# Two rounds of attention and FFN for four tokens on one core: shorter norm and row sums, q and every gate and up as shifted row strips, last down projection over four column groups, all orders new

## The chip, the cores and the metric

The kernel runs on one core of a Trainium2 chip. The metric is the device time of one execution in microseconds, taken as the median of several runs. Five engines work beside each other, each with an instruction queue of its own: TensorE (PE, with its weight loads shown as PEld), VectorE (DVE), ScalarE (ACT), GpSimd (POOL) and SyncE (SP). SP and ACT issue the transfers between memory and the core's buffers. An engine executes its queue in order, so an instruction that waits holds up everything behind it on that engine.

## The reference

Four tokens (B = 4, one position each, width D = 448) go twice through the same attention and the same FFN, with the same weights and the same caches in both rounds.

```python
def _A_ref(x, k_cache, v_cache, wq, wo):
    B, Sq, D = x.shape
    Hq, Dh = 16, 256
    Hkv, Sk = k_cache.shape[1], k_cache.shape[2]
    W = min(4096, max(256, Sk // 4))
...
    k = jnp.repeat(k_cache[:, :, Sk - W:, :], rep, axis=1)
    v = jnp.repeat(v_cache[:, :, Sk - W:, :], rep, axis=1)
    scores = jnp.einsum("bhqd,bhkd->bhqk", q, k) * (Dh ** -0.5)
    p = _softmax(scores, axis=-1)
    o = jnp.einsum("bhqk,bhkd->bhqd", p, v)
...
x = A_x
x = x + _A_ref(_layernorm(x, axis=-1), A_k_cache, A_v_cache, A_wq, A_wo)
x = x + _B_ref(_layernorm(x, axis=-1), B_w_gate, B_w_up, B_w_down)
x = x + _A_ref(_layernorm(x, axis=-1), A_k_cache, A_v_cache, A_wq, A_wo)
x = x + _B_ref(_layernorm(x, axis=-1), B_w_gate, B_w_up, B_w_down)
```

`_B_ref` is `(silu(x @ w_gate) * (x @ w_up)) @ w_down` with an inner width of 1792. There are 8 key/value heads, two query heads to each, a window W of 2048 keys and a head width of 256. One token and head therefore needs 1 MiB of K and 1 MiB of V.

## The kernel before

**Work items.** A head of one token in one layer is one item, written as three digits (token, layer, head). `PLAN` lists 44 stages of one to three items. For an item the kernel loads K in two halves of 512 KB (or one transfer of 1 MB, for items in `WHOLE`) and V in two halves. DVE transposes each K half in 32x32 blocks (L841), POOL spreads the query (L880), PE makes the scores (L874), a softmax runs over DVE, PE and ACT (L890 to L930), PE multiplies by V (L952), ACT and DVE fold the parts (L968, L970), and PE applies the output projection (rows, L1026, or columns, L1018, for the item that completes a token's layer).

**Buffers.** K and V halves live in 27 slots of 512 KB. `KEEP_K` and `KEEP_V` say how many heads of each token stay in their slots from the first layer to the second, so that they are not read twice: 21 heads of K and 18 of V in all, of which token 0 has 5 and 6. A load into a used slot waits for the last instruction that reads what the slot held. `SLOTS` gives the slot of each load, in the order of SP's queue. The weights have buffers of their own, `wq_sb` among them.

**Order.** All instructions are first collected in a graph with numbers; `SEQ_PE`, `SEQ_DVE`, `SEQ_ACT`, `SEQ_POOL` and `SEQ_SP` then give each engine's order by those numbers, and `schedule` and `_place_waits` add the waits. Entries `w1` to `w28` of `SEQ_PE` are fillers: a product with a zero vector over 512 columns (L1274), which changes nothing and keeps PE working. There are 339 of them.

**A token between two layers.** When all 8 heads of a token are done in layer 0, a chain follows that ends with the token's new queries. In this text it is called a *turn*; the four turns are T0 to T3, by token. Each goes through these steps:

- `rows`: the row sums of the output projection leave PSUM on ACT (L761, rounded to bf16), DVE makes the remainder (L763), PE turns both into columns (L771), DVE adds them to x (L775); the last item's column part is added by `residual` (L779).
- `norm`: two DVE sums with accumulation (L534, L537), a float32 product over the partitions on PE (L540), the centred x (L544), a copy of the moments (L546), the last 64 rows doubled (L548, L551), and three POOL instructions for the rate (L556, L558, L560).
- The FFN, in one of two forms. T0 and T3 use `ffn`, in columns: 56 products of a 128x128 weight block for gate and 56 for up (L720), tanh on ACT for each token (L731), L734 and L738 on DVE, 56 products for down (L748), and the sum into x (L756). T1 and T2 (`ROWF`) use `ffn_row`: gate and up as four groups of 4 rows by 512 columns (L656), tanh (L662), L664 and L666 over 512 columns, a turn to columns (L672), and the down projection added into the row sums in bank A (L684), so that `rows` has to run again for each token concerned. T2 takes token 0's second FFN along, T3 token 1's.
- `norm` again, and `qproj`: 32 products of 512 columns on four column groups (L594), two copies scaled by the rate (L600), two turns (L610), a copy (L617), a spread over the partitions (L625), and the copy to `qc` (L630).

**The end.** `finale` does the last FFN, for tokens 2 and 3, from a mean that is worked out ahead (L1051): centred x (L1073), its variance on PE (L1092) and the rate on POOL (L1098), gate and up in columns (L1117, L1128), tanh (L1149), L1152 and L1157, then x of all four tokens laid into rows (L1172) and the down projection of all 14 blocks in two column groups of 224 columns (L1182), one copy (L1188) and two stores with all four tokens (L1190).

## Time and profile before

| what | value |
|---|---|
| median of 3 runs | 287.29 us (287.08 to 287.34) |
| profiled execution, from first to last instruction | 290.4 us |
| instructions | 11178 |
| PE busy, of which fillers (L1274) | 251.9 us, 102.1 us |
| DVE busy, of which K transposes (L841) | 192.0 us, 105.4 us |
| ACT, POOL busy | 62.9 us, 82.8 us |
| read from memory | 105.48 MB |

The profile is of one execution with the profiler on; its span is 3.1 us above the timed median. A row of the timeline has the start and the length in us, the engine, the line of the kernel, the operation with what it writes and reads, the count of instructions merged in it and, in brackets, how long the engine sat idle before and what ended that. A row of the stretches has from:to, the length, the busy time of PE, PEld, DVE, ACT and POOL with their counts, the granted PE clock (1.00 is full speed), the mean busy share of the 16 transfer engines and the rate in GB/s.

### The profile page before, as it was taken

Reading aid. Unit: us, or ns where it says so; the run is one execution under the profiler, and the core shown is the slowest. Engines: PE = TensorE matmul, PEld = TensorE weight load, DVE = VectorE, ACT = ScalarE, POOL = GpSimd, SP = SyncE. Lnnn points to the kernel's source line nnn. Section 1 sums busy time; section 2 is a strip of 40 time slices with the busy share of each in tenths; the row PEclk is TensorE's granted clock in tenths of the full one; section 3 lists DMA queues with packets and bytes.
Section 4 is the critical chain, followed back from the end, with each engine's and each line's share of the span. In section 5 each row is a group of like instructions: output and inputs, shape, how many; then the busy total and the mean of one; then the engine's idle time right before and its main releaser. Section 6 shows DMA issues by size and latency. Waiting matters only on the chain.

```text
span 290.4 us, 11178 instructions
## 1 busy us (share of the span) xinstructions
PE 251.9 (87%) x4933; PEld 141.6 (49%) x4933; DVE 192.0 (66%) x594; ACT 62.9 (22%) x178; POOL 82.8 (29%) x233
## 2 busy tenths in 40 slices
PE   3989799899898999798989898988869988879976
PEld 1434344544474454354544544454536546745675
DVE  5527756547353895887867479959697679556532
ACT  0012011121202132213223122313323231223400
POOL 0071003031024224122423231605233162245231
PEclk9999889999999999999899999999999999999957
DMA  7999999999997999999999999999999999999800
GB/s 278 420 423 417 406 415 396 402 408 403 391 402 235 368 408 416 413 414 401 349 320 407 383 418 407 408 410 374 381 387 373 415 405 353 332 342 395 350 5 0
DMA packets 29192, 106.20 MB, mean 366 GB/s; under 512 B 2900, under 2 KB 7000, under 8 KB 26840
## 3 DMA queue, kind: packets, MB, share of 16 engines
q1 hardware_dynamic: 27424, 96.12, 85.3%
q10 hardware_dynamic: 1720, 9.37, 7.9%
q8 instruction: 38, 0.62, 0.9%
q14 instruction: 10, 0.08, 0.1%
HBM read 105.48 MB, written 0.00 MB: 363 GB/s over the span
## 4 chain that ended last, share of the span: by engine, by line
PE 42%; DMA 34%; DVE 16%; issue 2%; ACT 2%; SPq 2%; POOL 1%; DVEq 0%; ACTq 0%
DMA half<-in_A_k_cache_dram 29%; PE A L1274 13%; DVE half L841 10%; PE S L874 7%; PE Y L952 6%; DMA half<-in_A_v_cache_dram 5%; PE A L1026 2%; PE Z L720 2%; DVE oh L970 2%; PE Y L921 2%; PE Z L748 1%; ACT oh L968 1%; PE A L1018 1%; DVE tiny L890 1%; SPq L851 1%
## 5 line engine op out<-in xcount | busy, mean ns | idle before, releaser
L841 DVE STREAM_TRANSPOSE half<-half 128x1024 uint32<-128x1024 uint32 x86 | 105.4, 1233 | 12.2 <-DMA half<-in_A_k_cache_dram 12.1
L1274 PE MATMUL A<-identb,small 128*128 128x512 bf16 x339 | 102.1, 401 | 5.3 <-DVE A L434 4.8
L965 POOL TENSOR_TENSOR small<-small 128x2 f32<-128x2 f32 (+1 forms) x50 | 39.2, 789 | 57.3 <-DVE small L943 55.4
L952 PE MATMUL Y<-half,pT 128*4 128x256 bf16 (+1 forms) x992 | 43.3, 272 | 6.3 <-DMA half<-in_A_v_cache_dram 3.7
L874 PE MATMUL S<-half,qe 128*8 128x128 bf16 (+1 forms) x1600 | 41.6, 236 | 6.7 <-DVE half L841 2.3
L1274 PEld LDWEIGHTS A<-identb,small 128*128 128x128 bf16 x339 | 29.4, 104 | 33.1 <-issue 12.0
L874 PEld LDWEIGHTS S<-half,qe 128*8 128x8 bf16 x1600 | 28.9, 85 | 18.8 <-DVE half L841 4.5
L908 ACT ACTIVATE praw<-S,small 104x128 bf16<-104x128 f32 (+1 forms) x50 | 19.8, 397 | 82.2 <-DVE small L904 73.7
L880 POOL TENSOR_TENSOR qe<-qc,tiny 128x64 bf16<-128x64 bf16 x64 | 17.9, 293 | 51.1 <-PE S L874 37.5
L970 DVE SCALAR_TENSOR_TENSOR oh<-oh,small,Y 128x256 bf16<-128x256 bf16 x49 | 23.1, 472 | 13.4 <-ACT oh L968 12.9
L968 ACT ACTIVATE oh<-Y 128x256 bf16<-128x256 f32 x49 | 18.7, 382 | 49.0 <-PE Y L952 43.6
L952 PEld LDWEIGHTS Y<-half,pT 128*4 128x4 bf16 (+1 forms) x992 | 18.4, 83 | 17.8 <-DMA half<-in_A_v_cache_dram 5.4
L890 DVE TENSOR_REDUCE tiny<-S 104x1 bf16<-104x128 f32 (+1 forms) x50 | 15.9, 318 | 6.0 <-PE S L874 5.9
L930 ACT ACTIVATE pT<-Y 128x64 bf16<-128x64 f32 (+1 forms) x50 | 12.6, 252 | 33.0 <-PE Y L921 28.5
L1026 PE MATMUL A<-wo_sb,oT 128*4 128x448 bf16 x200 | 16.7, 352 | 1.8 <-DVE oT L1006 1.7
L556 POOL TENSOR_SCALAR st<-st 128x1 f32<-128x1 f32 x15 | 4.0, 265 | 48.0 <-DVE st L546 47.9
L904 DVE TENSOR_REDUCE small<-S 104x1 f32<-104x32 f32 x50 | 8.8, 179 | 11.8 <-PE S L898 11.4
L1212 POOL MEMSET oT<- 128x16 bf16 x40 | 4.1, 112 | 40.1 <-PE A L1026 30.5
L943 DVE TENSOR_REDUCE small<-Y 128x2 f32<-128x32 f32 (+1 forms) x50 | 9.3, 188 | 8.8 <-PE Y L938 8.5
L1006 DVE TENSOR_TENSOR oT<-Y,small 128x4 bf16<-128x4 f32 (+1 forms) x63 | 8.9, 154 | 6.8 <-PE Y L976 5.3
L976 PEld LDWEIGHTS Y<-tiny,oh 128*128 128x128 bf16 x98 | 6.7, 100 | 10.9 <-DVE oh L970 6.0
L976 PE MATMUL Y<-tiny,oh 128*128 128x2 bf16 (+1 forms) x98 | 9.7, 168 | 2.5 <-DVE oh L970 2.1
(181 smaller groups left out, 272.5 us busy)
## 6 DMA issues: line engine op xcount, KB each, us to landing
half<-in_A_v_cache_dram SPq DMA_DIRECT2D x90, 512.0 KB, 7.8
half<-in_A_k_cache_dram SPq DMA_DIRECT2D x55, 512.0 KB, 7.3
half<-in_A_k_cache_dram SPq DMA_DIRECT2D x10, 1024.0 KB, 13.5
half<-in_A_k_cache_dram ACTq DMA_DIRECT2D x5, 1024.0 KB, 23.4
wo_sb<-in_A_wo_dram SPq DMA_DIRECT2D x7, 448.0 KB, 16.0
wq_sb<-in_A_wq_dram ACTq DMA_DIRECT2D x2, 1024.0 KB, 8.8
wd_sb<-in_B_w_down_dram SPq DMA_DIRECT2D x1, 1568.0 KB, 15.6
wg_sb<-in_B_w_gate_dram SPq DMA_DIRECT2D x1, 1344.0 KB, 9.1
```

Source lines behind the costliest of these rows:

```text
L841: return e.transpose(a, a)
L874: last = e.matmul(Sb[s_][qd:qd + 8, 0:32 * 2 * J], lhsT=qe[q_][:, P, ce, :, :].rearrange("p a n -> p (a n)"), rhs=keys(kcs[P], J * x, J, c ...
L880: g.op(POOL, "qe", lambda e, P=P, t=t, kvh=kvh: e.tensor_tensor(qe[q_][:, P, :, :, :], qc[t][:, kvh, :, :].unsqueeze(2).broadcast_to([128, ...
L890: g.op(DVE, f"max{n}", lambda e: e.tensor_reduce(pmax[s_][0:R, :], Sb[s_][0:R, 0:N], AX.X, ALU.max), r=(f"s{s_}",), w=(f"pmax{s_}",), bank ...
L908: return e.activation(praw[0:R, 0:128 * n].rearrange("p (g r l) -> p g r l", g=2 * n, l=2), Sb[s_][0:R, 0:128 * n].rearrange("p (l g r) -> ...
L952: last = e.matmul(Yb[p_][32 * gg:32 * gg + M, 256:512], lhsT=pT[pt][:, gg, 2 * a + hv, 4 * P:4 * P + M] if n == 2 else p1[:, gg % 2, 2 * a ...
L965: g.op(POOL, f"pow{n}", lambda e: e.tensor_tensor(ri[p_][:, 0:2 * n], rs[p_][:, 0:2 * n], expo[:, 1:1 + 2 * n], op=ALU.pow), r=(f"rs{p_}", ...
L968: g.op(SCA, "oh", lambda e: e.activation(oh[:, :], Yb[p_][:, 256:512], ACT.Copy), r=(f"y{p_}",), w=("oh",), bank=(f"Y{p_}",))
L970: g.op(DVE, "oho", lambda e: e.scalar_tensor_tensor(out=oh[:, :], in0=oh[:, :], scalar=lomask[:, 0:1], in1=Yb[p_][:, 256:512], op0=ALU.mul ...
L976: last = e.matmul(Yb[p_][:, 2 * n * dh:2 * n * dh + 2 * n], lhsT=oh[:, :].rearrange("p (m e) -> p e m", e=2)[:, dh, :], rhs=osel[:, 0:2 * ...
L1026: last = e.matmul(Ab[32 * k:32 * k + B, 0:D], lhsT=oT[oi][:, k % 2, k // 2, :], rhs=wo_sb[:, 4 * kvh + k, :], start=False, stop=False, ski ...
L1274: return e.matmul(Ab[:, 0:512], lhsT=zero[:, 0:1].broadcast_to([128, 128]), rhs=identb[:, :].unsqueeze(1).broadcast_to([128, 4, 128]), sta ...
```

## The change

- **norm**: the sum of x comes out of the addition that makes x (`accum_out` of the residual), so one DVE sum goes (L534). The square sum is taken of x itself. PE's product uses 1/448 in place of 1. The copy of the moments becomes two small DVE instructions that make the variance per token (`nq`) and put it at the token's rows of a shared vector (`nm`). POOL is left with one power for the rate (`power`), the factors 1/2 and 1/4 being in that vector.
- **rows**: ACT copies the row sums in float32, and PE turns them with four float32 products. The remainder on DVE (L763) goes.
- **gate and up**, in every turn and in the end: x stands in a buffer with zeros around it, and a window of 16 columns that is shifted by 4 puts block 4j+i's result into rows 4i to 4i+3 of group j. One gate is 56 products of 128 columns on four column groups, and its result is 128 rows by 128 columns, so that tanh and the two DVE instructions behind it handle 128 columns once, for all tokens. The turn to columns is one product. `ffn_row` goes, and with it the second `rows`.
- **down** in the turns: 56 products with as many columns as tokens, onto x directly.
- **q**: 16 head strips of 256 columns in the same shifted form (64 products), one copy, one turn of 32 products, one copy to `qc` per token. The first chunk of the FFN's gate and of q is issued before the doubled rows are ready.
- **end**: the last FFN uses the same strips. The down projection goes over four column groups of 112 columns. Tokens 0 and 1 are laid into rows and stored before the last two stages; the last two stores carry tokens 2 and 3.
- **wq's buffer** becomes part of the K/V buffer: after the last q projection its 7 slots take seven loads of the last stages.
- **orders**: all five orders and the slots are new. PE has 542 instructions of the graph in place of 556 and 219 fillers in place of 339. The first entries of SP's new order are K and V loads, with x and the parts of wq after six of them. PLAN, KEEP_K, KEEP_V and WHOLE stay.

```diff
-        def norm(t, x):
...
+        def norm(t, x, key, mix, prev, bank):
+            zb, z, bk = bank
+            s, k = st[:, t, :], f"st{t}"
+            vec("nv", lambda e: e.scalar_tensor_tensor(out=s[:, 4:8], in0=x[:, t, :], scalar=1.0, in1=x[:, t, :],
                                                        op0=ALU.mult, op1=ALU.mult, accum_out=s[:, 1:2]),
...
+            vec("nxn", lambda e: e.tensor_scalar(xcol[:, 0:4, t], x[:, t, :], zb[:, 0:1], None, op0=ALU.subtract),
+                (key, z), (f"xn{t}",), (bk,))
+            vec("nq", lambda e: e.tensor_scalar(s[:, 2:3], zb[:, 0:1], zb[:, 0:1], zb[:, 1:2], op0=ALU.mult,
+                                                op1=ALU.subtract), (z,), (k + "q",), (bk,))
+            vec("nm", lambda e: e.scalar_tensor_tensor(out=mix, in0=nmk[:, t, :], scalar=s[:, 2:3], in1=prev,
...
+        def power(dst, key, src, n):
+            g.op(POOL, f"pr{n}", lambda e: e.tensor_tensor(dst, src[:, 0:n], expo[:, 0:n], op=ALU.pow),
...
+        def q_part(ts, c0, c1, kind):
...
+                for cc in range(c0, c1):
+                    for i in range(4):
                         for j in range(4):
...
+                            h = 4 * j + i
...
+                            last = e.matmul(Zb[32 * j:32 * j + 16, 0:256], lhsT=win(b, i), rhs=wq_sb[:, c:c + 256],
+                                            start=(cc == 0 and i == 0), stop=False, skip_group_check=True)
...
+        def gate_up(gi, c0, c1, kind):
...
+                            last = e.matmul(zb[32 * j:32 * j + 16, 0:128], lhsT=win(b, i), rhs=w[:, c:c + 128],
+                                            start=(cc == 0 and i == 0), stop=False, skip_group_check=True)
...
         def rows(t):
...
-            vec("rowsub", lambda e: e.tensor_tensor(wideb[:, 512:512 + D], Ab[:, 0:D], wideb[:, 0:D], op=ALU.subtract),
-                (f"row{t}", "wa"), ("wb",), ("A",))
...
+            g.op(SCA, "rowcp", lambda e: e.activation(wide[:, 0:D], Ab[:, 0:D], ACT.Copy), r=(f"row{t}",), w=WIDE + ("wh", "wt"),
...
+                    last = e.matmul(Zb[0:m, cc:cc + 1], lhsT=wide[:, 128 * cc:128 * cc + m], rhs=nmk[:, t, 0:1],
+                                    start=False, stop=False, skip_group_check=True)
...
             def down(e):
                 x = None
-                for f in fs:
-                    for i in range(2):
+                for f in range(NFC):
+                    for i in range(4):
                         x = e.matmul(ra[32 * i:32 * i + B, 0:W], lhsT=hc[:, f, :], rhs=wd_sb[:, f, W * i:W * i + W],
...
+            if si == len(PLAN) - EARLY:
+                g.tag = ("e",)
+                early([u for u in range(B) if done.get((u, 1)) == HKV and u not in waiting], gi)
...
+                gate_up(0, 0, 1, "g1")
+                extra(t, BZ)
+                gate_up(0, 1, 3, "g2")
+                gate_up(0, 3, 4, "gx")
+                gate_up(1, 0, 3, "g3")
+                gate_up(1, 3, 4, "gx")
+                late = ffn(ts, t)
+                norm(t, xr, f"x{t}", mixq, base, BZ2)
+                late()
+                power(rateq[:, 0:1], "rq", mixq, 1)
+                q_part([t], 0, 1, "qm1")
+                extra(t, BZ2)
+                q_part([t], 1, 3, "qm2")
+                lastq = q_part([t], 3, 4, "qmx")
+                q_rest([t])
```

More of the change, by code (lines that the diff above doesn't have):

```diff
@@ L37 @@
 KEEP_V = (6, 5, 4, 3)
-ROWF = (1, 2)
+EARLY = 2
 PLAN = (
@@ L248, in schedule @@
         last = {id(c): o for o in self.ops[:real] for c in o.rel}
-        held = [None] * npool
+        late = []
+        last[id(late)] = lastq
+        held = [None] * npool + [late] * 7
         slots = iter(SLOTS.split())
@@ new lines, in q_rest, with turn @@
+        def q_rest(ts):
+            n = len(ts)
+            g.op(SCA, "qcp", lambda e: e.activation(qrow, Zb[:, 0:256], ACT.Copy, scale=rateq[:, 0:1]), r=("z", "rq"),
+                 w=("wb",), bank=("Z",))
+            def turn(e):
+                last = None
+                for ce in range(8):
+                    w = qrow[:, 64 * (ce // 2):64 * (ce // 2) + 64].rearrange("p (s v) -> p v s", v=2)[:, ce % 2, :]
+                    for a in range(4):
+                        o = Z2[32 * a:32 * a + 32, 0:128 * n].rearrange("p (t x) -> p x t", t=n)
+                        last = e.matmul(o[:, 16 * ce:16 * ce + 16, :], lhsT=w, rhs=slots(ts), start=(ce == 0), stop=False,
@@ L676, in ffn_row @@
-            g.op(PE, "fturn", turn, r=WIDE + ("tsel",), w=("z",), bank=("Z",))
-            vec("fht", lambda e: e.tensor_copy(hT[:, :], Zb[:, 0:64]), ("z",), ("wb",), ("Z",))
-            def down(e):
-                last = None
-                for c in range(4):
-                    for j in range(4):
-                        if 4 * j + c < NFC:
-                            last = e.matmul(Ab[32 * j:32 * j + B, 0:D], lhsT=hT[:, 16 * c + 4 * j:16 * c + 4 * j + 4],
-                                            rhs=wd_sb[:, 4 * j + c, :], start=False, stop=False, skip_group_check=True)
-                return last
@@ new lines, in mm, with act_tanh, turn_h @@
+                return last
+            g.op(PE, kind, mm, r=(XN if c1 < 4 else XE) + (wk + ("a" if c1 < 4 else "b"),), bank=(bk,),
+                 **(dict(acc=(z,)) if c0 else dict(w=(z,))))
+        def act_tanh():
+            g.op(SCA, "tanhs", lambda e: e.activation(th, Z2[:, 0:128], ACT.Tanh, scale=ratef[:, 0:1]),
+                 r=("z2", "rf"), w=("wa",), bank=("Z2",))
+        def turn_h(n, ts):
+            def turn(e):
+                return e.matmul(Z2[:, 0:16 * n], lhsT=hrow, rhs=slots(ts), start=True, stop=True, skip_group_check=True)
+            g.op(PE, "fturn", turn, r=("wh", "identb"), w=("z2",), bank=("Z2",))
@@ new lines, in rows, with turn @@
+        def rows(t):
+            g.op(SCA, "rowcp", lambda e: e.activation(wide[:, 0:D], Ab[:, 0:D], ACT.Copy), r=(f"row{t}",), w=WIDE + ("wh", "wt"),
+                 bank=("A",))
+            def turn(e):
+                last = fresh(e, Zb[:, 0:4])
+                for cc in range(4):
+                    m = 128 if cc < 3 else 64
+                    last = e.matmul(Zb[0:m, cc:cc + 1], lhsT=wide[:, 128 * cc:128 * cc + m], rhs=nmk[:, t, 0:1],
+                                    start=False, stop=False, skip_group_check=True)
+                return last
+            g.op(PE, "rturn", turn, r=WIDE + ("wh", "wt", "nmk0", "identb", "inv"), w=("z",), bank=("Z",))
+            vec("rowadd", lambda e: e.scalar_tensor_tensor(out=xr[:, t, :], in0=Zb[:, 0:4], scalar=-0.25, in1=xs[:, t, :],
+                                                           op0=ALU.mult, op1=ALU.add), ("z", f"xs{t}"),
@@ L797, in build @@
+        for t in range(B):
+            norm(t, xs, f"xs{t}", mixq, base if t == 0 else mixq, BZ2)
+            extra(t, BZ2)
+        power(rateq[:, 0:1], "rq", mixq, 1)
+        q_part(list(range(B)), 0, 3, "qmm3")
+        q_part(list(range(B)), 3, 4, "qmm1")
+        q_rest(list(range(B)))
         seq = [p for s in plan() for b in s for p in b]
```

597 lines of the change are left out of this document (218 added, 379 removed), and 158 rows, old and new, of tables (SEQ_ACT, SEQ_DVE, SEQ_PE, SEQ_POOL).

## The prediction

> **What bounds the kernel now.** The page first: the span, and over 40 slices the rate of the transfers.
>
> ```profile
> span 290.4 us, 11178 instructions
> GB/s 278 420 423 417 406 415 396 402 408 403 391 402 235 368 408 416 413 414 401 349 320 407 383 418 407 408 410 374 381 387 373 415 405 353 332 342 395 350 5 0
> DMA packets 29192, 106.20 MB, mean 366 GB/s; under 512 B 2900, under 2 KB 7000, under 8 KB 26840
> ```
>
> Transfers run until the 38th slice of 7.26 us, that is to about 275 us, and then 15 us follow without them. The best slices reach 420 GB/s, but some fall to 235, 349, 320 and 332. The view of stretches, cut at those places, shows how much that is:
>
> ```profile
> 85.00:100.00 15.00, 13.78 (x310) 7.75 (x309) 9.15 (x32) 2.90 (x8) 4.52 (x12) 1.00 0.84 302
> 100.00:135.00 35.00, 31.52 (x635) 16.16 (x631) 27.68 (x65) 9.22 (x28) 9.62 (x25) 1.00 1.02 412
> 135.00:155.00 20.00, 17.43 (x311) 9.18 (x312) 15.29 (x45) 5.33 (x13) 6.99 (x21) 0.91 0.95 353
> 195.00:225.00 30.00, 25.25 (x601) 15.08 (x599) 24.18 (x63) 9.52 (x24) 11.36 (x33) 1.00 0.99 380
> 240.00:265.00 25.00, 21.38 (x598) 14.64 (x600) 17.29 (x57) 6.30 (x18) 8.82 (x26) 1.00 0.96 345
> ```
>
> Against the 412 GB/s of 100 to 135 us, the four others lose 15 x 110/412 = 4.0, 20 x 59/412 = 2.9, 30 x 32/412 = 2.3 and 25 x 67/412 = 4.1 us, together 13.3. These are shares of 27%, 14%, 8% and 16% of each stretch. All four lie at turns T0 to T3. Why the rate falls there is in SP's own waits and in its timeline:
>
> ```profile
> SPq L851 <- PE S L874: 35.0, 9, 17.0
> 67.83 20.95 SPq L851 DMA_DIRECT2D half<-in_A_v_cache_dram  x6
> ```
>
> SP stands at a load whose slot PE has not released; in 21 us it issues six loads. At T0, 5 heads of K and 6 of V of token 0, 22 of 27 slots, are held for its second layer and come free only when its new queries exist. So the bound is the transfer stream, interrupted by the turns, and after it the end chain.
>
> **The change, part by part: a turn.** T0 in the timeline:
>
> ```profile
> 76.12 0.54 ACT L761 ACTIVATE wide<-A 128x448 bf16<-128x448 f32 x1
> 76.70 0.62 DVE L763 TENSOR_TENSOR wide<-A,wide 128x448 bf16<-128x448 f32 x1
> 79.78 0.16 DVE L534 SCALAR_TENSOR_TENSOR st<-xr,small 128x4 f32<-128x4 f32 x1
> 80.25 0.34 PE L540 MATMUL Z<-st,small 128*128 128x2 f32 x2
> 80.93 1.48 PE L720 MATMUL Z<-xn,wg_sb 128*128 128x32 bf16 x42
> 84.61 0.27 ACT L731 ACTIVATE wide<-Z,st 128x14 f32<-128x14 f32 x1 [4.48 <-PE Z L720]
> 86.01 1.90 PE L748 MATMUL Z<-wide,wd_sb 128*128 128x32 bf16 x56
> 89.94 0.82 PE L594 MATMUL Z<-wq_sb,xn 128*4 128x512 bf16 x12
> 92.44 1.27 ACT L600 ACTIVATE wide<-Z,small 128x512 bf16<-128x512 f32 x2 [2.58 <-POOL small L565]
> 94.65 0.29 DVE L630 CAST qc<-Z 128x128 bf16<-128x128 f32 x1
> ```
>
> It takes 76.12 to 94.94, 18.8 us. No row shows the strips, but three have their shape: the scores are 64 products on four column groups of 128 or 256 columns, and the output columns are 128x128 weights against one column.
>
> ```profile
> 28.08 1.15 PE L874 MATMUL S<-half,qe 128*8 128x128 bf16 x64 [0.48 <-POOL qe L880]
> 258.85 2.04 PE L874 MATMUL S<-half,qe 128*8 128x256 bf16 x64 [0.63 <-POOL qe L880]
> 77.89 0.54 PE L1018 MATMUL A<-oT,wo_sb 128*128 128x1 bf16 x16
> ```
>
> - Row sums: the remainder (0.62) goes; the turn to columns, eight bf16 products, becomes four float32 ones. L540 is one float32 product, in two instructions, 0.34; four are some 1.2 (2.4 at half clock). I take +0.2, from -0.5 to +1.4.
> - Two norms lose one DVE sum each (79.78 to the next at 79.99): -0.4.
> - Gate to down: from 80.93 to tanh at 84.61 pass 3.7 us, since 42 products of up and the doubled rows stand before gate's last 14. Gate in strips is 56 of the 64 in 1.15, so 1.0, and 0.3 for the doubled rows: -2.4. From tanh to down (84.61 to 86.01, 1.4) now lie tanh, two DVE instructions of 128 columns, one product and one copy, 1.9 with up's end: +0.5.
> - Down: 56 products at the pace of L1018 (15 steps in 0.54 less 0.17 for the last, 25 ns each) 1.6, not 1.9: -0.2, as T3's is shorter already.
> - q: it starts behind the doubled rows and ends for ACT at 92.44, where POOL's rate came last (2.58 idle). In strips it is the 2.04 of L874 x64, its first chunk starts some 0.6 earlier, and the rate, one power behind two short DVE instructions, is there in time: -1.1.
> - Behind q: 92.44 to 94.94, 2.5 us, become a copy of 256 columns (half of L600's work), 32 products, one copy, some 1.6: -0.9.
>
> T0: -4.3 us. T3 has the same form: -4.3. T1 is of the row form:
>
> ```profile
> 142.17 0.69 ACT L662 ACTIVATE wide<-Z,small 128x512 f32<-128x512 f32 x1 [4.67 <-POOL small L636]
> 143.12 0.65 DVE L664 SCALAR_TENSOR_TENSOR wide<-wide,Z 128x512 f32<-128x512 f32 x1
> 143.87 0.75 DVE L666 SCALAR_TENSOR_TENSOR wide<-wide,small,Z 128x512 bf16<-128x512 f32 x1
> 149.56 0.16 DVE L779 TENSOR_TENSOR xr<-xr,A 128x4 f32<-128x4 f32 x1
> 204.87 0.54 ACT L761 ACTIVATE wide<-A 128x448 bf16<-128x448 f32 x1 [1.14 <-DVE xr L779]
> 206.71 0.16 DVE L779 TENSOR_TENSOR xr<-xr,A 128x4 f32<-128x4 f32 x1
> ```
>
> Tanh 0.69 to 0.3 (-0.4), 143.12 to 144.62 from 1.5 to 0.6 (-0.9); from there to 149.72 the turn, down and a second `rows` take 5.1, where one product, a copy, down 1.6 and a sum take 2.5 (-2.6); with norms, q and row sums as above (-2.2) T1 is -6.1. T2 also loses the second token's `rows`, 204.87 to 206.87: -8.1.
>
> What the stream gains has two bounds. If the low rate of each stretch only ends that much earlier, it is 27% of 4.3, 14% of 6.1, 8% of 8.1 and 16% of 4.3: 1.2 + 0.9 + 0.6 + 0.7 = **3.4 us**. If every gap closes, 13.3. I take the low end, since the slots still hang on the same kept heads. wq's seven slots take seven loads off the wait for slots after T3's q (about 256), so at most 9 us x 16% = 1.5; I take **0.6**.
>
> **The end.**
>
> ```profile
> 281.34 0.23 DVE L1073 SCALAR_TENSOR_TENSOR xn<-A,xr 128x4 bf16<-128x4 f32 x1 [1.41 <-PE Z L548]
> 282.81 0.59 PE L1092 MATMUL A<-st,small 128*128 128x1 f32 x2
> 284.44 0.27 ACT L1149 ACTIVATE wide<-Z,st 128x14 f32<-128x14 f32 x1 [0.27 <-POOL st L1098]
> 285.68 2.36 PE L1182 MATMUL Y<-wd_sb,wide 128*4 128x224 bf16 x28
> 288.08 0.38 DVE L1188 CAST wo_sb<-Y 36x224 bf16<-36x224 f32 x1 [2.26 <-PE Y L1182]
> 288.50 0.53 ACTq L1190 DMA_DIRECT2D out_dram<-wo_sb  x1
> ```
>
> From L1073 to tanh: two DVE instructions fewer ahead of the variance, one more behind it: -0.5. Tanh to down: one product and a copy more, +0.3. Down: 28 products of 224 columns on two groups are 3136 columns a group in 2.36; 56 of 112 on four are 1568, so 1.3: -1.0. By count of instructions (84 ns each) it would be 4.7, +2.3; the 18 ns each of L874 x64 speak for columns. The last copy is half as wide: -0.1. Together **-1.3**, from -2.3 to +1.3. The early stores cost nothing on the path if their copy finds DVE idle; they put two issues of 0.5 us on SP, and V's last half stands behind one of them.
>
> Where the covers are: six loads now go ahead of x and wq, some 4 MB, 10 us at 412 GB/s. Before, the 27 slots and wq, some 18 MB, keep the transfers full until about 45 us while the first scores come at 28.08, so a q that is 6 to 10 us late is hidden; past some 16 us it costs its excess. In that time DVE transposes.
>
> On the pace of the strips the Trainium skill speaks against the change: its page TensorE: Matmul & The Clock Gate, section "Wait — 56ns, not 53.3ns?", puts the distance of small matmuls at no less than about 25 ns. By it gate and up (112 products) would take an estimated 2.8 us a turn in place of 2.0, and the time would be 0.5 us longer; L874 x64 with 18 ns each disagrees.
>
> The sum: -3.4 - 0.6 - 1.3 = -5.3, so a span of 285.1. The profiled span is 3.1 above the timed median of 287.29, so **282.0 us**.
>
> **The rivals.**
>
> - The gaps mostly close (three quarters of 13.3, with the end): 276.0. For it speaks that the turns lose 22.8 us in all, more than the gaps; against it, that the kept slots are the same.
> - Nothing in the stream, since another wait ends as late (K to land, DVE's transposes: DVE is busy 27.7 of 35 us in 100 to 135): only the end, 286.0.
> - The clock. Fillers go from 339 to 219.
>
> ```profile
> 30.00:35.00 5.00, 3.00 (x48) 1.53 (x47) 4.46 (x8) 0.59 (x2) 0.29 (x1) 0.98 1.02 407
> 35.00:40.00 5.00, 4.32 (x21) 1.75 (x18) 1.71 (x6) 0.37 (x1) 0.00 (x0) 0.67 1.05 415
> 280.00:285.00 5.00, 4.70 (x157) 4.62 (x155) 1.36 (x11) 0.55 (x2) 2.88 (x9) 0.50 0.01 3
> ```
>
> After PE was busy for 3.0 of 5 us the granted clock was 0.67, at the end 0.50. A turn has some 8 us of PE work on its path (0.34 twice, 1.2, 1.0 twice, 1.6, 2.04, 0.5); at half clock that is up to 8 more, which eats the 4.3 to 8.1: no gain in the stream, a loss of 1.3, and the end's 1.3: 287.3. Against it: the new order keeps its fillers late, and drops about 100 of them ahead of the first tenth of the work, before q. The Trainium skill, page TensorE: Matmul & The Clock Gate, section "Why this matters for your kernels", warns of PE gaps over about 3 us, after which it gives half the clock; the 0.67 agrees with its direction.
> - Slower: SP's new order puts a load in front whose slot comes free late, and the loads behind it, whose slots are free, wait with it. Place: T0 and T3, where most slots are kept. Price: one gap like T0's is 4.0 us, two 8.0: 290.0. It decides from the point at which such waits outlast the loads already issued by 5.3 us in all.
>
> **How the numbers follow.** Forecast 0.50 (its own range 279.5 to 284.5), gaps close 0.14, only the end 0.15, clock 0.06, SP's order 0.15. The first three are faster by over 0.2%, 0.79, about what a measurement can tell from no change; the clock's case is the same, 0.06; SP's order is slower, 0.15. The range goes from 276.5 to 288.0: it leaves out half of the second case and most of the last.
>
> **What would show it.** Right: about 400 GB/s or more where the turns lie, turns of some 14 us from row copy to `qc`, tanh about 1.3 us behind the first gate product, down in the end about 1.3 us, no instruction like L763. Wrong: the same low slices with shorter turns (the stream hangs on something else), a clock below 0.9 at the turns, or long waits of SP with few loads issued.

## The result and the profile after

| kernel | median | lowest to highest | runs |
|---|---|---|---|
| before | 287.31 us | 287.08 to 291.73 | 4 |
| after | 321.19 us | 317.92 to 323.55 | 4 |

The changed kernel takes 1.115 times as long (95% interval 1.107 to 1.122), 33.9 us more. The forecast was 282.0 us with a range to 288.0: wrong in sign and far outside. The traces below are of single executions: that of the kernel before spans 290.4 us, and as the span of every other run lies 1.7 to 2.5 us below its time, it is one of an estimated 292 us, slower than the median, so that the two traces differ by 29.7 us and not by 33.9.

The page of the changed kernel: span, granted clock and transfer rate over 40 slices of 8.0 us, two rows of the queues (name, packets, MB, share), and the shares of the chain of work that ended last.

```profile
span 320.1 us, 11803 instructions
PEclk9999999999989999999699999997997978699998
GB/s 282 429 414 413 413 400 408 407 392 367 408 92 275 408 396 413 414 374 328 289 225 376 412 410 408 407 323 236 348 400 407 310 338 224 227 277 412 150 64 2
q8 instruction: 41, 0.67, 0.8%
PE 61%; DMA 17%; DVE 12%; issue 4%; ACT 3%; POOL 1%; SPq 1%; DVEq 0%; ACTq 0%
```

The same two rows of the kernel before:

```profile
q8 instruction: 38, 0.62, 0.9%
PE 42%; DMA 34%; DVE 16%; issue 2%; ACT 2%; SPq 2%; POOL 1%; DVEq 0%; ACTq 0%
```

The low slices at the turns, which were to become shorter, are deeper and longer (92, 225, 236, 224 GB/s). The chain has moved from transfers (34%) to PE (61%). And the transfers end at about 306 us, not 278. The view of stretches at the turns (from:to, length, busy times, then clock, transfer share, GB/s):

```profile
85.00:90.00 5.00, 5.00 (x120) 3.37 (x106) 0.91 (x4) 0.79 (x4) 0.18 (x1) 1.00 0.71 284
90.00:95.00 5.00, 5.00 (x71) 3.31 (x69) 0.84 (x8) 0.50 (x2) 0.00 (x0) 0.80 0.20 49
95.00:100.00 5.00, 4.60 (x173) 3.28 (x165) 1.04 (x5) 0.86 (x2) 1.91 (x7) 0.86 0.76 253
...
155.00:160.00 5.00, 5.00 (x45) 3.11 (x43) 1.49 (x9) 0.53 (x2) 0.00 (x0) 0.50 0.64 237
...
220.00:230.00 10.00, 9.94 (x244) 5.76 (x232) 5.75 (x17) 2.10 (x7) 2.85 (x6) 0.87 0.67 237
...
260.00:265.00 5.00, 5.00 (x78) 3.42 (x78) 3.50 (x12) 0.69 (x2) 0.88 (x3) 0.52 0.86 286
...
270.00:275.00 5.00, 4.25 (x73) 3.46 (x73) 1.71 (x5) 0.37 (x1) 0.00 (x0) 0.89 0.52 170
275.00:285.00 10.00, 9.69 (x210) 6.52 (x213) 4.67 (x19) 1.95 (x6) 2.39 (x7) 0.72 0.64 222
```

Around each turn PE is busy nearly all the time, at a clock that falls to 0.5 in places, and DVE, ACT and POOL have little to do. T0 in the timeline:

```profile
79.44 0.55 ACT L672 ACTIVATE wide<-A 128x448 f32<-128x448 f32 x1 [2.93 <-PE A L1163]
80.26 1.01 PE L679 MATMUL Z<-small,wide 128*128 128x1 f32 x8
84.28 1.07 PE L620 MATMUL Z<-wg_sb,xw 128*16 128x128 bf16 x56
86.05 0.37 ACT L627 ACTIVATE wide<-Z,small 128x128 f32<-128x128 f32 x1
88.15 3.98 PE L652 MATMUL Z<-wide,wd_sb 128*128 128x1 bf16 x56
94.16 1.07 PE L579 MATMUL Z<-half,xw 128*16 128x256 bf16 x16
95.28 1.99 PE L579 MATMUL Z<-half,xw 128*16 128x256 bf16 x48
97.33 0.47 ACT L588 ACTIVATE wide<-Z,small 128x256 bf16<-128x256 f32 x1 [2.40 <-PE Z L579]
98.34 0.29 DVE L602 CAST qc<-Z 128x128 bf16<-128x128 f32 x1 [2.59 <-PE Z L597]
```

T0 takes 79.44 to 98.63, 19.2 us instead of 18.8, and begins 3.3 us later. The four turns in both traces, from the start of the first row copy to the end of the last copy to `qc`, and the rate of the transfers in them:

| turn | before | after |
|---|---|---|
| T0 | 18.8 us, 331 GB/s | 19.2 us, 249 GB/s |
| T1 | 24.4 us, 362 GB/s | 26.5 us, 292 GB/s |
| T2 | 25.5 us, 392 GB/s | 24.3 us, 313 GB/s |
| T3 | 21.7 us, 347 GB/s | 26.1 us, 246 GB/s |

The turns are only 5.6 us longer together. But measured against the 412 GB/s that the kernel before reached from 100 to 135 us, the transfers miss an estimated 31.7 us in them, where they missed 11.3. As both kernels read the same bytes, these 20 us more have to be made up later, between the turns and behind them. T3's two rows, before and after:

```profile
236.47:258.17 21.70, 19.15 (x504) 12.71 (x504) 15.10 (x54) 5.39 (x17) 6.28 (x19) 1.00 0.96 347
256.90:283.01 26.11, 23.99 (x507) 17.38 (x499) 15.23 (x47) 4.09 (x12) 3.83 (x9) 0.74 0.71 246
```

In the timeline of T0, one row stands out: down (L652), 3.98 us for 56 small products. In T1 the same products are cut in two by something that is no wait:

```profile
150.69 2.02 PE L652 MATMUL Z<-wide,wd_sb 128*128 128x1 bf16 x28
154.57 2.24 PE L652 MATMUL Z<-wide,wd_sb 128*128 128x1 bf16 x28 [1.87 <-issue]
```

PE stands still for 1.87 us between the 28th and the 29th product of one loop; "issue" means that no event released it. So there are three suspects: the form of down's products (A), the clock (B), and these pauses (F). The rivals for the rest are SP's order (D) and the late start (G).

Three moments of the profiled executions divide the loss (the end of the last copy to `qc`, in T3; the start of the last row copy on ACT; the end of the span). Before:

```profile
257.88 0.29 DVE L630 CAST qc<-Z 128x128 bf16<-128x128 f32 x1 [0.50 <-PE Z L625]
275.92 0.54 ACT L761 ACTIVATE wide<-A 128x448 bf16<-128x448 f32 x1 [1.42 <-PE A L1026]
```

After:

```profile
282.71 0.29 DVE L602 CAST qc<-Z 128x128 bf16<-128x128 f32 x1 [1.95 <-PE Z L597]
306.95 0.54 ACT L672 ACTIVATE wide<-A 128x448 f32<-128x448 f32 x1 [1.65 <-PE A L945]
```

Up to the last copy of q 24.8 us are lost (283.0 against 258.2); from there to the last row copy 6.2 more (23.9 instead of 17.7); and behind it 1.3 are won (13.2 instead of 14.5).

**The pauses fall on code blocks.** Queue 8 moved 41 packets in 0.67 MB, 16 KB each. Counting PE's instructions (products and weight loads) from 0 in the order of their starts, every pause put down to issue of over a microsecond behind the first 45 us falls exactly on number 193 + 256 k, in both kernels, and PE goes on 2.2 to 2.5 us after a packet of queue 8 has started (the pause is given from the start of the instruction before it):

```
kernel    instruction   PE goes on   pause    packet started
after     4289  (k=16)  154.57 us    1.94 us  152.2
after     6593  (k=25)  219.54       1.19     217.3
after     8641  (k=33)  270.75       2.25     268.5
after     9409  (k=36)  289.94       1.43     287.5
after     9665  (k=37)  296.13       1.64     293.7
before    9409  (k=36)  277.80       1.34     275.5
```

So PE's code comes in blocks of 256 instructions, and a pause is a block that has not arrived. T1, T2 and T3 have one such pause each, T0 has none of over 0.4 us. The Trainium skill, page "Runtime: NRT & Kernel Launch", section "Instruction fetch mechanics", has blocks of 16 KiB or 256 instructions too, and calls the cost of a crossing "mostly hidden". For the size the trace agrees; hidden it is not here.

The next table is worked out from the traces in the same way: pauses of over 0.2 us at such crossings whose packet started 2.0 to 2.7 us before, and the time at half clock from 45 us to the end.

```
kernel                          PE instr.  last qc  last row copy  end    pauses  half clock
before                          9913       258.2    275.9          290.4   2.4    13.7
after                           10632      283.0    307.0          320.1   9.5    34.1
e1_sorted                       10632      272.9    297.6          310.7   8.6    34.1
e2_wide                         10632      268.6    294.7          308.7  13.3    17.6
e5_half_code                    9752       264.3    290.3          304.4   9.6    27.2
e11_start_strips                10102      260.2    286.2          300.3   7.9    13.7
e7_before_code                  11947      272.3    290.2          302.7  19.7    20.5
e15_before_code2                10591      260.7    281.4          293.8   7.8    23.9
```

### The profile page after: what moved, and what is told of

Read it like the earlier page. It is cut to its first block, busy times and chain, and to the rows that moved or that the text cites. A ratio compares the mean times of both kernels' runs of the same rounds, so it can differ in the third digit from the quotient of the medians.

```text
span 320.1 us, 11803 instructions
## 1 busy us (share of the span) xinstructions
PE 256.1 (80%) x5285; PEld 157.5 (49%) x5285; DVE 186.6 (58%) x575; ACT 56.1 (18%) x168; POOL 66.3 (21%) x176
## 4 chain that ended last, share of the span: by engine, by line
PE 61%; DMA 17%; DVE 12%; issue 4%; ACT 3%; POOL 1%; SPq 1%; DVEq 0%; ACTq 0%
DMA half<-in_A_k_cache_dram 15%; PE A L1163 14%; PE S L793 10%; PE Y L871 8%; DVE half L760 7%; PE Z L652 5%; PE Z L620 4%; PE Z L579 3%; DMA half<-in_A_v_cache_dram 3%; PE A L945 3%; PE Y L840 3%; PE Z L679 2%; PE A L937 2%; PE S L814 1%; DVE oh L889 1%
## 5 line engine op out<-in xcount | busy, mean ns | idle before, releaser
L1163 PE MATMUL A<-identb,small 128*128 128x512 bf16 x219 | 76.4, 417 | 3.5 <-DVE A L438 3.1
L793 PE MATMUL S<-half,qe 128*8 128x128 bf16 (+1 forms) x1600 | 45.4, 254 | 7.9 <-issue 3.1
L871 PE MATMUL Y<-half,pT 128*4 128x256 bf16 (+1 forms) x992 | 47.2, 283 | 2.1 <-DVE small L862 1.2
L884 POOL TENSOR_TENSOR small<-small 128x2 f32<-128x2 f32 (+1 forms) x50 | 39.1, 786 | 42.9 <-DVE small L862 42.1
L793 PEld LDWEIGHTS S<-half,qe 128*8 128x8 bf16 x1600 | 32.2, 91 | 18.2 <-issue 5.9
L1163 PEld LDWEIGHTS A<-identb,small 128*128 128x128 bf16 x219 | 19.1, 105 | 19.9 <-issue 11.6
L560 POOL TENSOR_TENSOR small<-small 128x1 f32<-128x1 f32 (+1 forms) x10 | 6.3, 628 | 103.9 <-DVE small L547 51.7
L887 ACT ACTIVATE oh<-Y 128x256 bf16<-128x256 f32 x49 | 18.8, 383 | 48.6 <-PE Y L871 31.1
L871 PEld LDWEIGHTS Y<-half,pT 128*4 128x4 bf16 (+1 forms) x992 | 17.7, 84 | 15.5 <-issue 7.8
L579 PE MATMUL Z<-half,xw 128*16 128x256 bf16 x320 | 14.4, 339 | 8.8 <-DVE xw L543 6.6
L945 PE MATMUL A<-wo_sb,oT 128*4 128x448 bf16 x200 | 17.6, 351 | 2.8 <-issue 1.4
L849 ACT ACTIVATE pT<-Y 128x64 bf16<-128x64 f32 (+1 forms) x50 | 12.5, 252 | 37.3 <-PE Y L840 25.5
L652 PE MATMUL Z<-wide,wd_sb 128*128 128x1 bf16 (+1 forms) x224 | 16.4, 175 | 1.9 <-issue 1.9
L652 PEld LDWEIGHTS Z<-wide,wd_sb 128*128 128x128 bf16 x224 | 14.4, 102 | 3.8 <-issue 1.8
L579 PEld LDWEIGHTS Z<-half,xw 128*16 128x16 bf16 x320 | 8.9, 108 | 11.7 <-DVE xw L543 6.7
```

Of the source, the lines that this page charges most:

```text
L579: last = e.matmul(Zb[32 * j:32 * j + 16, 0:256], lhsT=win(b, i), rhs=wq_sb[:, c:c + 256], start=(cc == 0 and i == 0), stop=False, skip_gro ...
L652: last = e.matmul(Zb[0:m, n * cc:n * cc + n], lhsT=wd_sb[:, f, 128 * cc:128 * cc + m], rhs=hT[:, n * f:n * f + n], start=False, stop=False ...
L793: last = e.matmul(Sb[s_][qd:qd + 8, 0:32 * 2 * J], lhsT=qe[q_][:, P, ce, :, :].rearrange("p a n -> p (a n)"), rhs=keys(kcs[P], J * x, J, c ...
L871: last = e.matmul(Yb[p_][32 * gg:32 * gg + M, 256:512], lhsT=pT[pt][:, gg, 2 * a + hv, 4 * P:4 * P + M] if n == 2 else p1[:, gg % 2, 2 * a ...
L884: g.op(POOL, f"pow{n}", lambda e: e.tensor_tensor(ri[p_][:, 0:2 * n], rs[p_][:, 0:2 * n], expo[:, 1:1 + 2 * n], op=ALU.pow), r=(f"rs{p_}", ...
L887: g.op(SCA, "oh", lambda e: e.activation(oh[:, :], Yb[p_][:, 256:512], ACT.Copy), r=(f"y{p_}",), w=("oh",), bank=(f"Y{p_}",))
```

## The experiments

Sixteen kernels ran; times are medians, each beside the kernel before on the same chip (287.9 to 289.5 us there). Where a ratio to the kernel before is given, its 95% interval stands behind it.

### Down's products (A and B)

**e1_sorted**:

```diff
-                for f in range(NFC):
-                    for cc in range(4):
-                        m = 128 if cc < 3 else 64
+                for cc in range(4):
+                    m = 128 if cc < 3 else 64
+                    for f in range(NFC):
```

> The changed kernel with the loops of the turns' down projection exchanged: all 42 products with 128 weight columns first, then the 14 with 64; the same products, the same order of everything else. Theory A (products of two weight widths in turn are slow; (3.98 - 1.57)/28 = 0.09 us per change of width, and late turns starve the transfers): down falls from 3.98 to about 1.6 us in T0, each of the four turns is 2.4 us or more shorter, and at least 15 of the 34 us come back: 306 us or less. Theory B (down keeps TensorE too idle and the granted clock falls behind it): down shortens a little, the slices with 0.5 to 0.9 behind each down stay, 312 us or more. Theory D (the order of SP's queue): no change, 319 to 323 us.

Measured: 316.7 us, ratio 1.096 (1.082 to 1.110). Down fell as expected:

```profile
87.43 1.72 PE L652 MATMUL Z<-wide,wd_sb 128*128 128x1 bf16 x56
```

But only 4.5 us of 34 came back, and the clock behind down still falls (e1, stretches):

```profile
90.00:95.00 5.00, 4.85 (x108) 2.90 (x112) 1.21 (x6) 0.97 (x3) 0.61 (x2) 0.66 0.57 212
```

Theory A is right about the row and wrong about the sum.

**e2_wide** adds to e1 the repeated column:

```diff
-                        last = e.matmul(Zb[0:m, n * cc:n * cc + n], ...
-                                        rhs=hT[:, n * f:n * f + n], ...
+                        last = e.matmul(Zb[0:m, 32 * cc:32 * cc + 32].rearrange("p (r t) -> p r t", t=n), ...
+                                        rhs=hT[:, n * f:n * f + n].unsqueeze(1).broadcast_to([128, 32 // n, n]), ...
```

> As the kernel with the sorted products, and besides each product's column is repeated to 32 columns, as the kernel before has it (TensorE streams 32 columns in place of 1 or 2). Theory B (one-column products let the granted clock fall): the clock behind each down stays at 0.95 or more, and the time is at least 5 us below that of the sorted kernel alone. Theory A alone: down some 1.9 us in place of 1.6, the time within 2 us of the sorted kernel's.

Measured: 311.2 us (306.4 to 312.7), 5.5 below e1, which meets what theory B asked of the time, but not what it asked of the clock. Down at T0 takes 2.02 instead of 1.72, and the fall of the clock there is gone; the one in T1 stays, right behind a pause. The stretches of e2:

```profile
90.00:95.00 5.00, 4.60 (x163) 3.10 (x167) 1.50 (x7) 1.35 (x4) 1.50 (x6) 1.00 0.72 221
145.00:150.00 5.00, 2.33 (x54) 1.75 (x53) 2.05 (x6) 0.38 (x1) 0.00 (x0) 1.00 1.01 398
150.00:155.00 5.00, 5.00 (x70) 2.98 (x68) 2.05 (x9) 0.59 (x2) 0.00 (x0) 0.66 0.64 232
```

And T2's pause in its timeline, 3.40 us:

```profile
213.31 1.02 PE L795 MATMUL S<-half,qe 128*8 128x128 bf16 x32 [3.40 <-issue]
```

**e4_before_mixed** puts A alone into the kernel before:

```diff
-                for cc in range(4):
-                    c0 = 128 * cc if cc < 3 else D - 128
-                    for fc in range(NFC):
-                        last = e.matmul(block(Zb, cc), lhsT=wd_sb[:, fc, c0:c0 + 128],
+                for fc in range(NFC):
+                    for cc in range(4):
+                        m = 128 if cc < 3 else 64
+                        last = e.matmul(block(Zb, cc)[0:m], lhsT=wd_sb[:, fc, 128 * cc:128 * cc + m],
```

> The kernel before with the changed kernel's order and widths in the down projection of its two column turns, T0 and T3: per block of the hidden vector three products with 128 weight columns and one with 64, in place of 56 with 128 sorted by output column; each still streams 32 columns. It leaves out part of the computation: 64 of the last 128 output columns are not set anew. Theory A: each of the two downs goes from 1.9 and 1.6 us to about 4.2, and the time rises by 1 to 4 us, to 288.5 to 291. Theory B alone (the one streamed column is what costs): both downs stay below 2.2 us, and the time stays at 287.3.

Measured: 297.1 us, ratio 1.032 (1.023 to 1.041), 8 us more by the medians: above what was expected from two downs. Down at T0 in its timeline:

```profile
84.35 5.00 PE L748 MATMUL Z<-wide,wd_sb 128*128 128x32 bf16 x56
```

The stretch behind it, with the clock at 0.54:

```profile
90.00:95.00 5.00, 5.00 (x47) 1.87 (x47) 0.63 (x6) 0.50 (x2) 2.77 (x7) 0.54 0.62 213
```

5.00 us against the old 1.90, each product streaming 32 columns: it is the change of weight width that costs, 28 times about 0.11 us, and the clock falls behind it as well. e1 and e4 also change the order of the output columns; the starts of the single products in the changed kernel's down at T0 tell the two apart. Between two products of 128 pass 25 ns, although the output column changes there too; from 128 to 64 it is 93 ns and from 64 to 128 it is 124 ns. In the profile these products are marked `128*64` beside `128*128`. The Trainium skill, page "TensorEngine Tiling (Array Packing)", section "Key Properties", says that changing the tiling mode drains TensorE; this run agrees with it and gives the size.

**e6_before_narrow**, one streamed column in the kernel before:

```diff
-                        last = e.matmul(block(Zb, cc), ..., rhs=more(hc[:, n * fc:n * fc + n]), ...
+                        last = e.matmul(block(Zb, cc)[:, 0, :], ..., rhs=hc[:, n * fc:n * fc + n], ...
```

> The kernel before, with each product of the down projection in its two column turns streaming one column in place of 32 equal ones; same order, same 128-wide weights, same values. Theory B (one-column products let the granted clock fall): a stretch of 3.4 us or more at half clock stands behind down at T0 and T3, and the time rises by 1 to 4 us. Rival (the clock falls for other reasons, such as the changes of weight width): no stretch at half clock there, time within 0.7 us of the kernel before.

Measured: 289.9 us, ratio 1.009 (1.004 to 1.013), some 2.5 us more, as theory B had it for the time and more than its rival's 0.7. The clock says otherwise. The stretches with its two downs:

```profile
85.00:90.00 5.00, 4.85 (x97) 2.50 (x98) 2.39 (x16) 0.50 (x2) 1.68 (x4) 1.00 0.98 365
...
245.00:250.00 5.00, 5.00 (x128) 3.91 (x128) 1.91 (x14) 0.87 (x3) 0.19 (x1) 0.56 0.72 271
```

Its timeline, down at T0 and what PE does ahead of down at T3:

```profile
84.29 1.55 PE L748 MATMUL Z<-wide,wd_sb 128*128 128x1 bf16 x56
...
244.98 0.61 PE L952 MATMUL Y<-half,pT 128*4 128x256 bf16 x16 [2.78 <-issue]
```

At T0 the clock stays at 1.00 with one column, so theory B in its plain form falls. At T3 the clock does fall (0.56), but from 245.6 us on, behind a pause of 2.78 us and ahead of down, which starts at 246.47. Most falls of the clock in these runs stand behind a pause of PE or behind a down with changing widths. That these set them off is not shown: in the changed kernel two stretches at half clock, from 243.1 and from 260.2 us, 10 us together, follow neither. Why 32 columns spare e2 the fall at T0 is not settled.

### Code (F)

**e7_before_code** and **e15_before_code2**, the fillers of the kernel before in four and in two pieces:

```diff
-            return e.matmul(Ab[:, 0:512], ..., rhs=identb[:, :].unsqueeze(1).broadcast_to([128, 4, 128]), ...
+            for i in range(4):
+                x = e.matmul(Ab[:, 128 * i:128 * i + 128], ..., rhs=identb[:, :], ...
```

> The kernel before with each of its 339 fillers issued as four products of 128 columns instead of one of 512: the same columns, 2034 instructions of PE more (about 8 code blocks of 256). Theory F: some crossings of 193 + 256 k show idle times of 1 us or more, and the time rises by 2 us or more. Rival (code loading keeps up with anything that streams 128 columns): no idle time above that of the kernel before (1.34 us, at instruction 9409), time within 1 us.

> The kernel before with each of its 339 fillers issued as two products of 256 columns: the same columns, 678 instructions more, close to the 719 that the change adds. At 8 ns an instruction (16.3 us for 2034): 5.4 us more, 293 us. Rival: code costs only where it is dense, and single pairs of products are hidden: within 1.5 us of the kernel before.

Measured: e7 304.3 us, ratio 1.049 (1.037 to 1.061); e15 295.1, ratio 1.031 (1.023 to 1.040). The same columns, and 16.3 us more by the medians for 2034 instructions; 678 instructions, about as many as the change adds (719), cost 5.6 us by the medians and 9 by the ratio. The split itself occupies PE little longer: in a run of fillers at full clock, one follows the other after 215 ns whole, 218 in two pieces and 224 in four, which is 1 and 3 us for all 339. From the page of e7, its code packets and the shares of its chain:

```profile
q8 instruction: 46, 0.75, 1.0%
...
PE 66%; DVE 15%; issue 7%; DMA 6%; ACT 3%; POOL 2%; POOLq 0%; DVEq 0%; ACTq 0%
```

One of its pauses, between fillers, in the timeline:

```profile
62.27 0.33 PE L1275 MATMUL A<-identb,small 128*128 128x128 bf16 x3 [1.41 <-issue]
```

Between its crossings lie mostly 5.6 to 6.7 us, however many fillers stand in them: some 24 ns an instruction, 48 ns a product. Single blocks are passed faster (4.0 and 4.5 us in e7).

**e5_half_code** (on e2) and **e8_wide_strips** (on e2, with the reference's values) take code away:

```diff
-                    for i in range(4):
+                    for i in range(0, 4, 2):
...
-                            last = e.matmul(zb[32 * j:32 * j + 16, 0:128], lhsT=win(b, i), rhs=w[:, c:c + 128],
+                            last = e.matmul(zb[32 * j:32 * j + 16, 0:256], lhsT=win(b, i), rhs=w[:, c:c + 256],
```

> As the kernel with sorted and 32-column down products, and besides gate, up and q of each turn (and gate and up of the end) are issued as half as many products of twice the columns: 28 of 256 instead of 56 of 128, 32 of 512 instead of 64 of 256. The same number of weight columns is streamed, in about 176 instructions of PE fewer a turn. It computes other values in half of the blocks, so gate, up and q are not the reference's. Theory F (PE's code arrives in blocks of 256 instructions, and small products use it up faster than it is loaded: the idle times of 1.3 to 3.4 us without a releaser, all at instruction 193 + 256 k): these idle times go or fall below 0.7 us, T1 and T2 are each 3 us or more shorter, and the time is 8 us or more below that kernel's 311. Rival (the idle times have another cause, such as a wait that the profile doesn't show): they stay at the same products, and the time changes by less than 3 us.

> As the kernel with sorted and 32-column down products, with gate and up in strips of 256 columns that yield the reference's values: 29 products in place of 56 each, tanh and the two DVE steps on 256 columns, the turn to columns in two products; q stays at 64. Some 106 instructions fewer a turn, DVE and ACT some 0.4 us a turn more. Theory F: T1's and T2's idle times shrink by at least half, the time falls by 4 us or more below 311. Rival: no fall, or a rise by the 1.6 us that DVE and ACT add.

Measured: e5 305.4 us, ratio 1.060 (1.052 to 1.068), 5.8 below e2 where 8 were expected; T1's pause is gone and T2's is 1.3 us instead of 3.4, but others of 1.4 to 2.3 us come around T3 and behind it, and all pauses sum to 9.6 us instead of 13.3. e8 309.7 (302.0 to 311.9), 1.5 below e2, which its spread does not tell from nothing. So fewer instructions seem to help, but no version here got rid of the pauses; they moved to other stretches. And the count alone can't be the cause of the rest: e5 has fewer instructions on PE than the kernel before (9752 against 9913) and is still 6% slower.

### The start (G), the fillers, and both

**e9_start** (on e2) puts x and q's weights ahead of K and V in SP's order, and the first twelve transposes behind the norms in DVE's. **e11_start_strips** has the same and e8's strips. **e10_no_fillers** is e2 without the `w` entries of PE's order.

> As the kernel with sorted and 32-column down products, with the start as the kernel before has it: in SP's order x and q's four weight parts stand ahead of all K and V loads, and in DVE's order the twelve first transposes of K stand behind the norms of the four tokens, not between them; PE's order is untouched. Theory G (the late start costs what is left: first scores at 44 us instead of 28, and PE, short of code, can't catch up): first scores at 32 us or earlier, T0 3 us or more earlier, time 304 us or less. Rival (the late start is hidden, as the prediction has it, since the transfers are full until T0 in both): first scores earlier, but the time within 3 us of 311.

> The start of the kernel before (as above) together with the strips of 256 columns for gate and up; the reference's values. If both the late start and the code cost time: 302 us or less. If only one of them does: the better of the two alone, within 3 us. The kernel before, 288 us, is beaten by neither theory.

> As the kernel with sorted and 32-column down products, without any of its 219 fillers: 438 instructions of PE fewer, and PE idle where they stood. Theory F, in its strong form (from T0 on PE is paced by its code, 24 ns an instruction as in the kernel before with four times the fillers): the time falls by 4 us or more, to 307 or less. Rival (the fillers hold the clock): stretches at half clock multiply and the time rises by 3 us or more.

Measured: e9 311.6 us, no gain, though its first `qc` comes 4 us earlier (39.1 against 43.3) and that of T0 2 us (92.1 against 94.0). The edit did less to the start than was expected: the norms end at 19 us, but the first copy to `qc` still stands behind the twelve transposes in DVE's order, which wait for K until 38.9 us. So the test is weak; as far as it goes, the late start is hidden. e11 306.0, ratio 1.064 (1.051 to 1.077), within what e8 spreads over. e10 318.5, ratio 1.103 (1.093 to 1.112), 7 us above e2; its clock:

```profile
PEclk9999999999577559967795597985965786599756
```

The rival held: the fillers keep the clock up (without them it is half for 119.5 us from 45 us on, against 17.6 in e2), and they are worth more than their code costs.

### The stretch behind the last turn (D, and its fillers)

**e3_stores** (on the changed kernel) and **e12_tail_stores** (on e11) move SP's last V load ahead of the two early stores; **e13_tail_fillers** takes the twelve fillers between T3's q and the end's gate out of e11; **e14_tail_both** does both.

> The changed kernel with SP's last V load moved ahead of the two early stores in SP's order, nothing else. Theory D (SP stands 13.5 us at an early store, and V's last half, the end's last transfer, behind it): V's last half is issued some 13 us earlier, at about 289 us instead of 302.9, and the time is 5 to 10 us shorter: 311 to 316 us. Rival (PE reaches the last values no earlier, since its order has 14 us of other work before them): within 1 us of the changed kernel, 320 to 322 us.

> The kernel with the old start and the strips of 256 columns (306.0), with SP's last V load moved ahead of the two early stores. Theory D: V's last half is issued some 5 us or more earlier, and the time falls by 2 us or more. Rival: PE reaches the last values no earlier, within 2 us of 306.

> The same kernel (306.0), without the twelve fillers between the last turn's q and the end's gate products. If they stand on the path (12 times 0.2 us and 24 instructions of code): 2 to 4 us less. Rival: they fill waits or hold the clock: within 1 us, or up to 4 us more with longer stretches at half clock.

> Both of these edits. If either is hidden behind the other (V's last half late, PE's order late): 3 us or more below the better of the two alone. Otherwise the sum of the two.

Measured: e3 323.2 (318.8 to 326.7), ratio 1.114 as without it. e12 303.0, e13 307.3, e14 305.8, against 306.0 (302.2 to 311.8) for e11: e12's 3 us less are within these spreads, and e14 doesn't repeat them. In the traces the stretch from the last `qc` to the last row copy stays at 25.6 to 26.1 us in all four; where e13 leaves the fillers out, half clock in it grows from 3.4 to 10.0 us. In e11, whose transfers are nearly back in step (last `qc` at 260.2 against 258.2), the chain of that stretch runs through PE almost without a wait for another engine, with two pauses for code, and PE comes late to the last scores:

```profile
264.43 1.04 issue
...
269.65 2.02 issue
...
276.97 0.88 PE S L780 x16
...
282.57 0.31 PE Y L827 x8
...
285.59 0.56 PE A L932 x8
```

From `qc` to these scores pass 16.8 us and from them to the row copy (286.20) 9.2; before, it is 11.8 and 5.9 (L874 at 270.01, in the timeline). Between them stand, in PE's order, the row sums, output columns and rows of the tokens that are stored early. The traces of e11 and of the kernel before give the parts of the 8.3 us by which this stretch is longer: PE is busy 6.4 us more (22.5 instead of 16.0) and idle 1.9 more. In the busy part are ten fillers, 3.3 us, where the kernel before has none, 3.4 us at half clock, and some 65 products more; in the idle part are the two pauses, where the kernel before has 0.18 us. That fits with the new order of PE as the cause, and code as a part of it. It was not tried: an order of PE for this stretch as the kernel before has it.

### The end's down alone

**e16_before_end** is the kernel before with `W = D // 4` and four groups in the end's down projection.

> The kernel before with the end's down projection over four column groups of 112 columns (56 products) in place of two of 224 (28 products), and so four stores of 112 columns in place of two of 224, two on SP and two on ACT; all else as it was. The forecast's term (columns count): down 0.9 to 1.3 us in place of 2.36, the copy 0.1 less, the second store of each queue 0.5 more, together 0.6 to 1.1 us less than the kernel before. Theory F (56 more instructions at 24 ns in a tail that is short of code): down about 2.2 us, no gain or 0.5 us more.

Measured: ratio 0.998 (0.994 to 1.003), no difference that can be told; the interval, from 1.8 us less to 0.8 more, also holds the 0.6 to 1.1 less that were expected. In the trace down shrinks from 2.36 to 1.54 us, where 0.9 to 1.3 were expected and the columns say half (the clock is mostly at 0.50 in both), and the second stores take part of it back:

```profile
284.16 1.54 PE L1168 MATMUL Y<-wd_sb,wide 128*4 128x112 bf16 x56
285.76 0.28 DVE L1174 CAST wo_sb<-Y 100x112 bf16<-100x112 f32 x1 [1.27 <-PE Y L1168]
286.06 0.84 ACTq L1176 DMA_DIRECT2D out_dram<-wo_sb  x2
```

## Why the prediction was wrong

- **The step that failed: "Down: 56 products at the pace of L1018 ... 1.6, not 1.9: -0.2".** It is 3.98 at T0 and 4.06 in T3's chain. The pace itself was right for products of one width (1.55 in e6, 1.72 sorted in e1). The step overlooked that every fourth product has 64 weight columns behind three of 128, and that each change costs about 0.1 us. Sorted, 4.5 us come back; with 32 columns, 10.0 of 33.9.
- **What no step counted: code.** The strips were priced by columns, and where they run unhindered the price held: gate 1.07 (forecast 1.0), q 2.2 in e2 (forecast 2.04). But a turn issues some 280 small products, where the old forms issue about 240 (T0, T3) or 130 (T1, T2), and the code did not always come in time. The page showed queue 8 with its 38 packets, and 1.18 us of PE's idle time in the old end was just such a pause. The 719 more instructions cost some 6 to 9 us, if they cost what e15's 678 did, and the pauses rise from 2.4 to 9.5 us.
- **"The clock ... Against it: the new order keeps its fillers late"** was too light. The clock was half for 34.1 us instead of 13.7 behind the first 45; at most half of the 20.4 us more, 10, is lost by it. Whether the 120 fillers fewer, which the rival had named, have a part in it was not tried; leaving out the other 219 cost 7 us (e10). In e11's trace, of an execution of 302.2 us, the clock is half for 13.7 us, as before, so what is left there is not the clock.
- **The stream's term** (-3.4) took each turn to be 4.3 to 8.1 us shorter. T1 grew to 26.5 us and T3 to 26.1, only T2 shrank, by 1.2, and the transfers starved at all four. But the step fails where turns do get shorter, too. In e11's trace they take 16.0, 20.8, 21.4 and 18.8 us, 13.4 less together than before, for which the forecast's own shares give some 2 us. The mean rate up to the last `qc` is 382 GB/s there, 386 before and 351 in the changed kernel, and that `qc` comes 2.0 us later than before. So shorter turns won nothing in the stream, as the rival "Nothing in the stream" had it; which wait ends as late is not known.
- **Right by themselves**: row sums (1.01 for the four products, forecast 1.2), the steps behind q (97.33 to 98.63, 1.3; forecast 1.6), tanh to down (2.1, forecast 1.9). Gate to tanh is 1.8, not 1.3.
- **The end was right by luck.** Behind the last row copy 1.3 us are won, and the forecast was 1.3. But from centred x to tanh nothing is won (3.2 us instead of 3.1; forecast -0.5), from tanh to down 0.9 are lost (forecast 0.3), and the last copy and the stores cost 0.4 more. What makes up for it is the pause of 1.18 us, which is not there any more, and down, which wins 1.5 us instead of 1.0, because the clock is at 1.00 in its row and half for most of the old one. At nearly the same clock, in e16, it wins 0.8:

```profile
316.49 0.86 PE L1062 MATMUL Y<-wd_sb,wide 128*4 128x112 bf16 x56 [0.28 <-DVE wide L1053]
```

- **The late start was sized wrongly**: first scores at 44.08 instead of 28.08, 16 us and not 6 to 10. It seems hidden, as said: taking 4 us of it away won nothing (e9); the other 12 were not tried.
- **The rival that was to be slower, SP's order at 290.0**, had the right sign and the wrong mechanism: SP does stand 13.5 us at an early store ahead of V's last half, and moving it showed no difference.
- **What stays open.** The best version with the reference's values, e12, is at 303.0, still 5.9% (4.6 to 7.3) above the kernel before; none beats it. Of the 24.8 us up to the last `qc`, e11's trace (302.2 us) has 2.0 left, against a trace of the kernel before that is itself slower than its median; the edits of down, strips and start together bring the rest, and their shares are not separated. In the same trace 8.3 us lie between the last `qc` and the last row copy. The runs exclude stores and fillers as their main cause; the order of PE and code fit, and are argued, not shown. No run has the new products in the old orders, so what the new orders cost by themselves is not known. The shares don't add up strictly, since a pause can also cost clock.

## What to carry to other kernels

Price small products three times: by columns, by changes of weight shape between neighbours, and by the number of instructions per microsecond against the pace at which code arrived in a trace. Sort products so that one weight width runs through before the next begins. In a kernel that is bound by transfers, PE's slack pays for its pauses; a change that adds instructions to the stretches on which slots wait spends that slack where it is dearest.

## What the runs showed of the hardware

- PE's code arrives in blocks of 256 instructions, in packets of 16 KB. PE went on 2.2 to 2.6 us after the packet's start in every pause of over a microsecond; with code short throughout (e7), mostly 5.6 to 6.7 us pass for a block, 24 ns an instruction. Splitting each filler in four at the same columns made the kernel 4.9% slower, though the fillers themselves took only some 3 us longer.
- Alternating 128 and 64 weight columns costs about 0.1 us a change: 3.98 against 1.72 us for the same 56 products. From start to start it is 25 ns from 128 to 128, 93 from 128 to 64 and 124 from 64 to 128.
- One streamed column in place of 32 takes 1.55 instead of 1.90 us for 56 products, and the clock needn't fall for it (e6, T0).
- Taking out 219 fillers, 438 instructions, cost 7 us: here the clock was dearer than the code.
